# A linear-attention block with adaptive norm: the running sum and the modulation sums of the token loop go from VectorE to GpSimd and ScalarE

## The chip, the cores and the metric

The kernel runs on one core of a Trainium2 chip. What counts is the time of one execution on the device in microseconds; the median of several runs is given. A core has five engines that work side by side, each through its own list of instructions in order: TensorE (PE in the profile, its weight loads PEld), VectorE (DVE), ScalarE (ACT), GpSimd (POOL) and SyncE (SP, which here issues most of the DMAs). They wait for one another by semaphores.

## The reference, cut to what matters

There are 2048 tokens of width D = 512, in float32. A vector c gives six modulation vectors; a block of linear attention with 32 heads of 16 follows, then a bilinear feed-forward part.

```python
mod = (_silu(c) @ w_mod).reshape(c.shape[0], 6, 1, -1)
sa, ca, ga, sb, cb, gb = (mod[:, 0], mod[:, 1], mod[:, 2], mod[:, 3], mod[:, 4], mod[:, 5])
h = _layernorm(x, axis=-1) * (1 + ca) + sa
x = x + ga * _A_ref(h, A_wqkv, A_wo)
h = _layernorm(x, axis=-1) * (1 + cb) + sb
x = x + gb * _B_ref(h, B_w_gate, B_w_up, B_w_down)

# in _A_ref
phi = lambda t: jnp.where(t > 0, t + 1, jnp.exp(t)) + 1e-6
pq, pk = phi(q), phi(k)
kv = jnp.einsum("bhsd,bhse->bhde", pk, v)
z = jnp.einsum("bhsd->bhd", pk)
num = jnp.einsum("bhqd,bhde->bhqe", pq, kv)
den = jnp.einsum("bhqd,bhd->bhq", pq, z)[..., None] + 1e-6
```

Two sums matter here. z is the sum of phi(k) over all tokens. And each modulation vector is a product of silu(c), 512 long, with a 512x512 part of w_mod.

## The kernel before

The tokens are worked on in four chunks of 512, each of four tiles of 128 tokens by 512 columns, so sixteen tiles. Matrix products are made from pairs: a matrix is split into a high part, rounded to the format that TensorE takes, and a low part, the rest, and three matmuls (high by high, high by low, low by high) make one product. ScalarE writes most high parts, VectorE subtracts to get the low ones.

The kernel has a first part (norm and modulation of the first chunk), then a token loop, and then the attention's second half and the feed-forward part. The token loop goes over the tiles i = 4 to 15, after tiles 0 to 3 written out before it. In one step i of the loop

- TensorE makes the projection to k of tile i + 2 (`proj`, twelve matmuls of 128x512 on lines 219 to 221); the last two steps project q of tiles 4 and 5 instead, and step 4 also projects q of tile 3;
- ScalarE and VectorE split the normed x of tile i + 1 (`k_split_x`: xh, xl, lines 206 and 207) and its phi(k) (`k_split`: kh on line 363, kl on line 364);
- two of the first steps of each chunk transpose and modulate the next chunk (`transpose`, line 284; `modulated`, lines 302 to 307), whose pair h, l the later projections read;
- ScalarE and VectorE make phi(k) of tile i + 2 from the projection (`k_phi`, lines 327, 328 and 331);
- VectorE adds phi(k) of tile i + 1 to the running sum `zacc` (`z_add`, line 357; line 355 for the first);
- TensorE adds the products of tile i to four accumulators that stay in place over the whole loop (`t_tile`, lines 372 to 374, twelve matmuls of 128x512);
- and what `extra[i]` lists for this step: weight splits, loads, and the modulation vectors.

Modulation vectors 2 to 5 are made in the loop, beside the tokens. For vector v, `mod_load` fetches four pieces of w_mod of 128x512, and `mod_part(v, ...)` lets VectorE build the tile `accs[v]`: piece 0 times its column of silu(c) (line 178), then for pieces 1 to 3 a multiply and add (line 180). What remains is a sum over the 128 partitions, which TensorE makes: with ones as a column for vectors 3 and 4 (`mod_col`, line 185, then `col_out` on VectorE), or, for vectors 2 and 5, from a split pair with a block of ones (`mod_row`, line 195, copied out by ScalarE). After the last tile the running sum is split as well, and TensorE sums it over the partitions (`over_rows`, line 195). GpSimd's only work in the loop is the power that gives a chunk's reciprocal deviation (line 262); right after the loop it multiplies phi(q) by the summed z (line 712).

The order of instructions of each engine is the order in which the program writes them: the schedule is manual. Tiles of 128x512 come from one pool of 99 buffers, and an instruction that gets a buffer waits until the last reader of what was in it is done. Four PSUM banks serve the projections, transposes and column sums in turn, and four hold the accumulators.

Of the kernel before, what the change touches and what calls it, by code (L numbers as in the profile page):

```python
# [10 lines left out]
AF = mybir.ActivationFunctionType  # L11
ALU = mybir.AluOpType
# [10 lines left out]
def tile_adaln_block(  # L23
# [12 lines left out]
    nc = tc.nc  # L36
# [33 lines left out]
    def T(p, tag, shape=(P, D), dt=F32, bufs=None):  # L70
        cnt[0] += 1
        return p.tile(list(shape), dt, tag="t" if p is tiles else tag, name=f"{tag}_{cnt[0]}", bufs=bufs)

    def B(tag, shape=(P, D), dt=F32):

        return T(tiles, tag, shape, dt)
# [4 lines left out]
    def bank():  # L81
        return T(ps_w, "bank")
# [26 lines left out]
    def load(src, tag, by=None):  # L109
        raw = B(tag, (P, *src.shape[1:]))[:src.shape[0]]  # L110
        (by or nc.sync).dma_start(raw, src)
        return raw
# [44 lines left out]
    sc = consts.tile([P, KD], F32, name="sc")  # L157
# [14 lines left out]
    def mod_acc(acc, raws, ks, on=None):  # L172
        for k in ks:
            if k == 0:
                if on:
                    on.activation(acc, raws[k], AF.Copy, scale=sc[:, 0:1])
                else:
                    nc.vector.tensor_scalar(acc, raws[k], sc[:, 0:1], None, op0=ALU.mult)
            else:
                nc.vector.scalar_tensor_tensor(acc, raws[k], sc[:, k:k + 1], acc, op0=ALU.mult, op1=ALU.add)  # L180

    def mod_col(acc, ps):

        for b in range(KD):
            nc.tensor.matmul(ps[:, b:b + 1], acc[:, b * P:(b + 1) * P], ones, start=True, stop=True)
        return ps

    def col_out(v, ps, add):
        t = consts.tile([P, KD], F32, name=f"col{v}")
        nc.vector.tensor_scalar(t, ps[:, :KD], add, None, op0=ALU.add)  # L190
        return t

    def over_rows(ps, pair):
        for m, x in enumerate(pair):
            nc.tensor.matmul(ps, ones_r, x, start=m == 0, stop=m == 1)

    def mod_row(v, pair):
        ps = bank()
        over_rows(ps, pair)
        t = consts.tile([P, D], F32, name=f"row{v}")  # L200
        nc.scalar.activation(t, ps, AF.Copy)
        return t


    def split(src, h, l, low=None):
        nc.scalar.activation(h, src, AF.Copy)  # L206
        (low or nc.vector).tensor_tensor(l, src, f32(h), op=ALU.subtract)  # L207

    def split_raw(raw, shape=(P, D), low=None):
        h = B("w", shape, F32R)  # L210
        l = B("w", shape, F32R)
        split(raw, h[:raw.shape[0]], l[:raw.shape[0]], low)
        return h, l
# [99 lines left out]
    NT = NCH * NJ  # L313
    norm = [Norm(xts[0])]
    wk, wq, wv = [], [], []
    kx, phk, phq, q_ps = {}, {}, {}, {}
# [36 lines left out]
    def z_add(i):  # L353
        if i == 1:
            nc.vector.tensor_tensor(zacc, phk[0], phk[1], op=ALU.add)
        elif i > 1:
            nc.vector.tensor_tensor(zacc, zacc, phk[i], op=ALU.add)
        phk.pop(i - 1, None)

    def k_split(i):  # L360
# [23 lines left out]
    zacc = B("z")  # L384
# [188 lines left out]
    rows, cols = {}, {}  # L573
    accs = {}

    raw_m, raw_o, wo_s = {}, [], []
# [2 lines left out]
        raw_m.update({v: load_mod(v) for v in vs})  # L579

    def mod_part(v, *ks):
        if 0 in ks:
            accs[v] = B("f")
        mod_acc(accs[v], raw_m[v], ks)

    extra = {4: lambda: (wv.extend(split_raw(r) for r in raw_v[0:1]),),
             5: lambda: (wv.extend(split_raw(r) for r in raw_v[1:2]),),
             6: lambda: (wv.extend(split_raw(r) for r in raw_v[2:3]), mod_load(2),),
             7: lambda: (wv.extend(split_raw(r) for r in raw_v[3:4]),),
             8: lambda: (mod_part(2, 0, 1), mod_load(3)),  # L590
             9: lambda: (mod_part(2, 2, 3), mod_load(4)),
             10: lambda: (accs.update({2: split_raw(accs[2])}), mod_part(3, 0, 1, 2), mod_load(5)),
             11: lambda: (mod_part(3, 3), mod_part(4, 0, 1), rows.update({2: mod_row(2, accs[2])})),
             12: lambda: (raw_o.extend(load(wo_v[k], "raw") for k in range(KD)), mod_part(4, 2, 3), mod_part(5, 0), cols.update({3: col_out(3, mod_col(accs[3], bank()), 0.0)})),
             13: lambda: (mod_part(5, 1, 2, 3), wo_s.extend(split_raw(x) for x in raw_o[:1]), accs.update({5: split_raw(accs[5])}), cols.update({4: col_out(4, mod_col(accs[4], bank()), 1.0)})),
             14: lambda: (wo_s.extend(split_raw(x) for x in raw_o[1:]),), 15: lambda: rows.update({5: mod_row(5, accs[5])})}
    q_at = {4: 3}
    ahead = {}

# [15 lines left out]
    t_tile(1, *range(KD))  # L615
    qps2 = proj(2, wq)
    z_add(1)
    k_split_x(3)
    nx.transpose(0, 1)
# [5 lines left out]
    nx.transpose(2, 3)  # L625
    nx.modulated(ca, sa, 2, 3, cast=nc.vector)
    z_add(2)
    q_a(2, qps2)
    q_b(2)
    z_add(3)  # L630
    t_tile(3, *range(KD))
    ahead[4] = proj(4, wk)
# [971 lines left out]
```

## Time and profile before

| | |
|---|---|
| median of 3 runs | 554.61 us (554.56 to 554.82) |
| span of the profiled execution | 552.4 us, 2.2 us less than the median |
| TensorE matmuls, busy | 545.8 us (99%), granted clock 0.999 |
| TensorE weight loads | 460.1 us (83%) |
| VectorE | 432.2 us (78%) |
| ScalarE | 299.5 us (54%) |
| GpSimd | 176.8 us (32%) |
| stretch 88 to 122 us of the token loop | TensorE 34.00, VectorE 29.96, ScalarE 18.35, GpSimd 0.00 of 34.00 us |

The span goes from the first to the last instruction of the one execution that was profiled; the time of a run also holds what lies around it, 554.61 − 552.4 = 2.2 us. The token loop of steps 4 to 15 lies between about 55 and 127 us. Busy shares are averages over stages with different limits, so the stage of the change is read by itself. A line of a timeline gives the start in us, the duration, the engine, the line of the code, the operation, and what is written from what; in brackets stands how long the engine was idle before and what ended that. A line of groups gives the number of instructions, their busy time and the mean of one in ns, then the idle time before them. For a single line of the code the three numbers are the shortest, the median and the longest in ns.

### The profile page before, as it was taken

Reading aid. Unit: us, or ns where it says so; the run is one execution under the profiler, and the core shown is the slowest. Engines: PE = TensorE matmul, PEld = TensorE weight load, DVE = VectorE, ACT = ScalarE, POOL = GpSimd, SP = SyncE. Lnnn points to the kernel's source line nnn. Section 1 sums busy time; section 2 is a strip of 40 time slices with the busy share of each in tenths; the row PEclk is TensorE's granted clock in tenths of the full one; section 3 lists DMA queues with packets and bytes.
Section 4 is the critical chain, followed back from the end, with each engine's and each line's share of the span. In section 5 each row is a group of like instructions: output and inputs, shape, how many; then the busy total and the mean of one; then the engine's idle time right before and its main releaser. Section 6 shows DMA issues by size and latency. Waiting matters only on the chain. (4 is left out here: it accounts for less than half of the span.)

```text
span 552.4 us, 8146 instructions
## 1 busy us (share of the span) xinstructions
PE 545.8 (99%) x2775; PEld 460.1 (83%) x2775; DVE 432.2 (78%) x794; ACT 299.5 (54%) x535; POOL 176.8 (32%) x180
## 2 busy tenths in 40 slices
PE   8999999999999999999999999999999999999997
PEld 6888888888888888888888888878888888888886
DVE  6878779978998998865655767797577877879696
ACT  4876857456467876654545355463243534453540
POOL 2000000003527646353556644540002524242400
PEclk9999999999999999999999999999999999999999
DMA  8910224203230045195888634289786534342004
GB/s 256 373 57 1 76 77 152 77 0 77 78 115 2 0 154 189 39 316 180 285 286 274 222 123 163 87 312 391 231 259 218 173 131 138 129 146 86 1 0 153
DMA packets 58512, 83.24 MB, mean 151 GB/s; under 512 B 6564, under 2 KB 23720, under 8 KB 58472
## 3 DMA queue, kind: packets, MB, share of 16 engines
q1 hardware_dynamic: 56544, 81.16, 44.1%
q10 hardware_dynamic: 1928, 1.58, 0.9%
q8 instruction: 22, 0.36, 0.3%
q14 instruction: 18, 0.15, 0.1%
HBM read 53.02 MB, written 29.69 MB: 150 GB/s over the span
## 5 line engine op out<-in xcount | busy, mean ns | idle before, releaser
L1057 PE MATMUL bank<-h,w 128*128 128x512 f32 (+1 forms) x924 | 221.6, 391 | 0.2 <-POOL w L1020 0.2
L1057 PEld LDWEIGHTS bank<-h,w 128*128 128x128 f32 (+1 forms) x924 | 168.2, 186 | 36.2 <-POOL w L1020 0.6
L1063 ACT ACTIVATE bank<-bank 128x512 f32<-128x512 f32 (+2 forms) x46 | 26.2, 571 | 122.7 <-PE bank L1057 122.5
L1253 DVE TENSOR_TENSOR x<-acc,x 128x256 f32<-128x256 f32 x132 | 48.0, 414 | 13.7 <-PE acc L1226 13.1
L1226 PE MATMUL acc<-w,kh 128*128 128x256 f32 x308 | 57.1, 282 | 0.0
L1226 PEld LDWEIGHTS acc<-w,kh 128*128 128x128 f32 x308 | 50.6, 190 | 3.7
L1020 POOL TENSOR_TENSOR w<-raw,w 128x256 fp32r<-128x256 f32 (+3 forms) x22 | 24.7, 1121 | 73.7 <-ACT w L1013 64.1
L219 PE MATMUL bank<-w,h 128*128 128x512 f32 x112 | 44.1, 394 | 0.0
L221 PE MATMUL bank<-w,h 128*128 128x512 f32 x112 | 43.7, 390 | 0.0
L220 PE MATMUL bank<-w,h 128*128 128x512 f32 x112 | 43.6, 390 | 0.0
L1226 PE MATMUL acc<-w,kl 128*128 128x256 f32 x154 | 43.5, 283 | 0.0
L871 PE MATMUL acc<-w,xh 128*128 128x512 f32 x128 | 40.7, 399 | 0.0
L712 POOL TENSOR_TENSOR f<-h,zb 128x512 f32<-128x512 f32 x12 | 17.5, 1468 | 62.9 <-ACT zb L692 48.9
L262 POOL TENSOR_TENSOR rstd<-ve,half 128x4 f32<-128x4 f32 (+3 forms) x12 | 11.2, 935 | 81.4 <-DVE ve L259 68.0
L1083 DVE TENSOR_TENSOR phi<-bank,g 128x512 f32<-128x512 f32 (+1 forms) x22 | 15.1, 687 | 25.2 <-PE bank L1057 25.2
L1063 ACT ACTIVATE u<-bank 128x512 f32<-128x512 f32 (+1 forms) x44 | 26.1, 594 | 15.4 <-PE bank L1057 15.2
L1113 DVE TENSOR_TENSOR g<-bank,u 128x512 f32<-128x512 f32 (+1 forms) x22 | 15.2, 689 | 21.2 <-ACT u L1063 19.9
L1020 POOL TENSOR_TENSOR w<-t,w 128x512 fp32r<-128x512 f32 (+1 forms) x22 | 29.6, 1346 | 0.0
L1146 PE MATMUL acc<-w,kh 128*128 128x512 f32 (+1 forms) x76 | 29.6, 390 | 0.0
L1147 PE MATMUL acc<-w,kh 128*128 128x512 f32 (+1 forms) x76 | 29.6, 390 | 0.0
L1148 PE MATMUL acc<-w,kl 128*128 128x512 f32 (+1 forms) x76 | 29.6, 389 | 0.0
L277 ACT ACTIVATE n<-x,nmr,rstd 128x512 f32<-128x512 f32 x31 | 23.6, 808 | 10.9 <-DVE nmr L267 10.7
(204 smaller groups left out, 1187.0 us busy)
## 6 DMA issues: line engine op xcount, KB each, us to landing
right<-w SPq DMA_DIRECT2D x56, 256.0 KB, 3.7
w<-right SPq DMA_DIRECT2D x56, 256.0 KB, 4.3
x<-in_A_x_dram SPq DMA_DIRECT2D x22, 256.0 KB, 5.2
raw<-in_w_mod_dram SPq DMA_DIRECT2D x22, 256.0 KB, 3.7
raw<-in_B_w_down_dram SPq DMA_DIRECT2D x18, 256.0 KB, 3.0
side_s<-h SPq DMA_DIRECT2D x16, 256.0 KB, 2.6
h<-side_s SPq DMA_DIRECT2D x16, 256.0 KB, 5.3
raw<-in_A_wqkv_dram SPq DMA_DIRECT2D x12, 256.0 KB, 6.2
```

The lines of the kernel that those rows point to most:

```text
L219: nc.tensor.matmul(ps, ah, bh, start=begin and i == 0, stop=False)
L220: nc.tensor.matmul(ps, ah, bl, start=False, stop=False)
L221: nc.tensor.matmul(ps, al, bh, start=False, stop=end and i == n - 1)
L871: nc.tensor.matmul(yps[i], x, y, start=fresh and k + n == 0, stop=k == KD - 1 and n == 2, skip_group_check=True)
L1020: sub = lambda out, x, y: (on or nc.gpsimd).tensor_tensor(out, x, f32(y), op=ALU.subtract)
L1057: mm = lambda x, y, **kw: nc.tensor.matmul(ps, x[:, k], y, skip_group_check=True, **kw)
L1063: nc.scalar.activation(out, x, AF.Copy)
L1146: nc.tensor.matmul(dn[j], hh[:n, a:b], dh[:n], start=i == 0, stop=False)
L1147: nc.tensor.matmul(dn[j], hh[:n, a:b], dl[:n], start=False, stop=False)
L1148: nc.tensor.matmul(dn[j], hl[:n, a:b], dh[:n], start=False, stop=i == n_of - 1)
L1226: mm = lambda x, y, **kw: nc.tensor.matmul(ps, x[:, a:b], y, skip_group_check=True, **kw)
L1253: nc.vector.tensor_tensor(xt[:, halves[at]], banks[b][m], xt[:, halves[at]], op=ALU.add)
```

## The change

The addition to the running sum goes to GpSimd for tiles 5 to 13; tiles 1 to 4, 14 and 15 stay on VectorE. Each of the sixteen modulation pieces (four vectors of four) is multiplied by ScalarE into a tile of its own; the first piece's tile becomes `accs[v]`, and GpSimd adds the other three to it, twelve additions in all. The split of `accs[5]` moves from step 13 to step 14 of the loop, behind the weight splits of that step.

```diff
         elif i > 1:
-            nc.vector.tensor_tensor(zacc, zacc, phk[i], op=ALU.add)
+            on = nc.gpsimd if 4 < i < NT - 2 else nc.vector
+            on.tensor_tensor(zacc, zacc, phk[i], op=ALU.add)
...
     def mod_part(v, *ks):
-        if 0 in ks:
-            accs[v] = B("f")
-        mod_acc(accs[v], raw_m[v], ks)
+
+        for k in ks:
+            part = B("f")
+            nc.scalar.activation(part, raw_m[v][k], AF.Copy, scale=sc[:, k:k + 1])
+            if k:
+                nc.gpsimd.tensor_tensor(accs[v], accs[v], part, op=ALU.add)
+            else:
+                accs[v] = part
...
-             13: lambda: (mod_part(5, 1, 2, 3), wo_s.extend(split_raw(x) for x in raw_o[:1]), accs.update({5: split_raw(accs[5])}), cols.update({4: col_out(4, mod_col(accs[4], bank()), 1.0)})),
-             14: lambda: (wo_s.extend(split_raw(x) for x in raw_o[1:]),), 15: lambda: rows.update({5: mod_row(5, accs[5])})}
+             13: lambda: (mod_part(5, 1, 2, 3), wo_s.extend(split_raw(x) for x in raw_o[:1]), cols.update({4: col_out(4, mod_col(accs[4], bank()), 1.0)})),
+             14: lambda: (wo_s.extend(split_raw(x) for x in raw_o[1:]), accs.update({5: split_raw(accs[5])})), 15: lambda: rows.update({5: mod_row(5, accs[5])})}
```

## The prediction

> **What bounds the kernel now.** I read four views: the page's busy times, the list of waits of TensorE, the table by stretch of the token loop, and then the order of time around the places where TensorE takes a result of VectorE just after it is made. First the page.
>
> ```profile
> span 552.4 us, 8146 instructions
> PE 545.8 (99%) x2775; PEld 460.1 (83%) x2775; DVE 432.2 (78%) x794; ACT 299.5 (54%) x535; POOL 176.8 (32%) x180
> ```
>
> TensorE is busy for all but 552.4 − 545.8 = 6.6 us. Busy time of a pipelined engine can hide short stalls, so the waits and the start times have to confirm it. These are all the waits of TensorE's matmuls that the trace lists:
>
> ```profile
> PE acc L153 <- DVE w L148: 2.0, 1, 2.0
> PE bank L295 <- ACT n L277: 0.6, 1, 0.6
> PE bank L1057 <- POOL w L1020: 0.2, 1, 0.2
> ```
>
> None is on a line of the token loop (projections L219 to L221, products of the sum L372 to L374). The loop, over the two stretches that the change touches. After the length stand the busy us and instructions of PE (TensorE's matmuls), PEld, DVE (VectorE), ACT (ScalarE) and POOL (GpSimd), then TensorE's granted clock, the DMA share and GB/s:
>
> ```profile
> 56.00:88.00 32.00, 32.00 (x154) 26.62 (x153) 25.01 (x48) 25.07 (x41) 1.24 (x2) 1.00 0.31 99
> 88.00:122.00 34.00, 34.00 (x163) 28.38 (x163) 29.96 (x52) 18.35 (x31) 0.00 (x0) 1.00 0.19 62
> ```
>
> The reader should see TensorE at 34.00 of 34.00 us at a granted clock of 1.00, although VectorE is at 29.96. VectorE is crowded but it is not what TensorE waits for. Now the start times of two projections, each of 12 matmuls of 128x512 (first row of each, and the row that follows its last):
>
> ```profile
> 96.87 0.39 PE L219 MATMUL bank<-w,h 128*128 128x512 f32 x1
> ...
> 99.59 0.39 PE L372 MATMUL acc<-kh,xh 128*128 128x512 f32 x1
> ...
> 102.78 0.40 PE L219 MATMUL bank<-w,h 128*128 128x512 f32 x1
> ...
> 105.54 0.39 PE L372 MATMUL acc<-kh,xh 128*128 128x512 f32 x1
> ```
>
> (99.59 − 96.87)/12 = 0.227 us from start to start, (105.54 − 102.78)/12 = 0.230. So hidden stalls are at most some 0.04 us in a projection. In this loop TensorE sets the time, and work taken from VectorE is taken from beside it.
>
> **What is removed.** Nine of the fifteen additions of the running sum (tiles 5 to 13), and sixteen modulation products, leave VectorE:
>
> ```profile
> L357 DVE TENSOR_TENSOR z<-z,phi 128x512 f32<-128x512 f32 x14 | 9.5, 682 | 0.0
> L180 DVE SCALAR_TENSOR_TENSOR f<-raw,sc,f 128x512 f32<-128x512 f32 x12 | 9.0, 750 | 0.3
> ...
> L178 DVE TENSOR_SCALAR f<-raw,sc 128x512 f32<-128x512 f32 x4 | 1.9, 482 | 0.0
> ```
>
> 9 × 0.682 + 9.0 + 1.9 = 17.0 us. On the path: 0, because no matmul of the loop waits for VectorE.
>
> **What is added on ScalarE.** Sixteen scaled copies of 128x512. The trace has no such copy in that shape, only these neighbours: a plain copy, and an activation with a scale and a bias from SBUF.
>
> ```profile
> L206 ACT ACTIVATE xh<-n x15: 613/616/631, 31.6 to 142.0; 128x512 fp32r<-128x512 f32 x15
> ```
> ```profile
> L277 ACT ACTIVATE n<-x,nmr,rstd 128x512 f32<-128x512 f32 x31 | 23.6, 808 | 10.9 <-DVE nmr L267 10.7
> ```
>
> One operand from SBUF instead of none or two: between 0.616 and 0.808, I take the middle, 0.71; sixteen make 9.9 to 12.9, taken as 11.4 us. All fall behind the activation at 86.49 us that is quoted below, where ScalarE would go from 18.35 to about 29.7 of 34 us (31.3 at the upper end). It fits. What lies behind a product on ScalarE is the next tile's split and the exponentials; they cost nothing while the free time in that stretch covers them.
>
> **What is added on GpSimd.** Twenty-one additions (9 of the sum, 12 of the products) of two 128x512 operands. The nearest row has the same shape:
>
> ```profile
> L712 POOL TENSOR_TENSOR f<-h,zb x12: 1277/1306/1837, 125.9 to 215.4; 128x512 f32<-128x512 f32 x12
> ```
>
> 1.306 as a rule, 1.837 at worst: 27.4 us, up to 38.6. GpSimd is nearly empty here (1.24 and 0.00 us above). Seventeen of them fall in the stretch of 34 us (sum tiles 9 to 13 and the twelve): 22.2 us, at worst 31.2. It fits, but the consumers on TensorE have to be looked at one by one.
>
> **The new waits.** TensorE takes the columns of vector 4 in loop step 13, and the row of vector 5 in step 15; these are the latest additions against the earliest use.
>
> ```profile
> 86.49 0.63 ACT L328 ACTIVATE phi<-phi 128x512 f32<-128x512 f32 x1
> ...
> 121.79 1.66 ACT L206 ACTIVATE w<-raw 128x512 fp32r<-128x512 f32 x3
> ```
> ```profile
> 114.66 0.95 PE L185 MATMUL bank<-ones,f 128*128 128x1 f32 x8
> ...
> 127.00 0.62 PE L195 MATMUL bank<-w,ones_r 128*128 128x512 f32 x2
> ```
> ```profile
> 122.53 1.89 DVE L207 TENSOR_TENSOR w<-raw,w 128x512 fp32r<-128x512 f32 x3
> ```
>
> The first two products stand behind the activation of 86.49 and are done at 87.12 + 2 × 0.71 = 88.5. From there to the last addition of vector 4 GpSimd has 13 additions: 9 of products (an addition for each of k = 1 to 3 of vectors 2, 3 and 4) and 4 of the sum (tiles 10 to 13). At the worst duration, one straight after the other, they end at 88.5 + 13 × 1.837 = 112.4, before 114.66. The three of vector 5 then end at 117.9. Its split was moved to step 14: on ScalarE it stands behind the three weight copies that end at 123.45, so GpSimd is done 5 us before. On VectorE its low half follows the three that end at 124.42 and takes 0.69 more: 125.1, against a use at 127.00. Vectors 2 and 3 end earlier in the same queue; a split of vector 2 that waits for GpSimd holds up ScalarE, behind it the next products and the split of the next tile, whose use is one loop step (105.54 − 99.59 = 5.95 us) later. VectorE's addition for tile 14 now waits for GpSimd's for tile 13, the eleventh of the 13, done by 88.5 + 11 × 1.837 = 108.7 at worst; in the order of the program it comes after phi of tile 15, whose row follows.
>
> ```profile
> 113.43 0.69 DVE L331 SCALAR_TENSOR_TENSOR phi<-bank,phi 128x512 f32<-128x512 f32 x1 [1.99 <-ACT phi L328]
> ```
>
> So it finds its operand ready by 5 us; were it late, the rest of step 13 on VectorE would stand behind it. Cost of all these waits: 0.
>
> **The two tight places.** VectorE's results reach TensorE with the least to spare here: the low half of phi(k) of tile 8, and the low half of the last chunk's fourth block (first its making, then the first matmul that reads it).
>
> ```profile
> 80.55 0.68 DVE L364 SCALAR_TENSOR_TENSOR kl<-phi,kh 128x512 fp32r<-128x512 f32 x1
> ...
> 92.66 0.69 DVE L307 TENSOR_TENSOR h<-f,h 128x512 fp32r<-128x512 f32 x1
> ```
> ```profile
> 81.91 0.39 PE L374 MATMUL acc<-kl,xh 128*128 128x512 f32 x1
> ...
> 93.93 0.39 PE L221 MATMUL bank<-w,h 128*128 128x512 f32 x1
> ```
>
> To spare: 81.91 − 81.23 = 0.68 us and 93.93 − 93.35 = 0.58. Both have sum additions of VectorE ahead of them that go (tiles 6 and 7 before the first; tile 9 and two products, 0.68 + 0.48 + 0.75 = 1.9 us, before the second), so left alone they gain room. But GpSimd now runs at the same time, and the trace shows what that does to VectorE:
>
> ```profile
> 180.99 1.28 POOL L1020 TENSOR_TENSOR w<-t,w 128x512 fp32r<-128x512 f32 x1
> ```
> ```profile
> 181.05 1.27 DVE L735 TENSOR_TENSOR den<-den,den 128x32 f32<-128x32 f32 x1
> ```
> ```profile
> L735 DVE TENSOR_TENSOR den<-den,den x12: 191/194/1270, 156.5 to 231.0; 128x32 f32<-128x32 f32 x12
> ```
>
> An addition of 0.194 us took 1.270 and ended 0.05 us after GpSimd's instruction: it had been held until GpSimd was through. The price of one encounter is between 0 (it falls beside an instruction that is not held) and 1.28. Most of VectorE's work in the loop reads two SBUF operands, so I count half an instruction of GpSimd, 0.64, for each of the two that can meet VectorE ahead of each place: 1.28. Against it stand the room of 0.68 + 2 × 0.68 = 2.0 and 0.58 + 1.9 = 2.5. Stall taken: 0. If each encounter costs a whole 1.28 and nothing were gained before: 2 × 1.28 − 0.68 = 1.9 and 2 × 1.28 − 0.58 = 2.0, together 3.9 us; this is the upper end.
>
> The same rows give a second upper end, by the stretch instead of the place. Of 88 to 122 us, 9.0 + 1.9 + 5 × 0.68 = 14.3 us leave VectorE, and if each of the 17 additions holds it for a whole 1.28, 21.8 come back: 29.96 − 14.3 + 21.8 = 37.5 of 34 us, so the loop would end 3.5 us later.
>
> The Trainium skill, SBUF — State Buffer, section "Who interferes with whom", has this as a rule: a VectorE instruction with two SBUF inputs and a GpSimd instruction that reads SBUF exclude each other for the whole of the one that came first. The row of 1.270 agrees with it. By the rule at its hardest the sum would be the 3.5 us of the stretch, by the rows at half an encounter it is 0.
>
> **Buffers.** Twelve more tiles of the pool of 99 are taken, so later loads get other buffers, and a load waits until its buffer's last reader is through. The SP queue shows such a wait ahead of the loads of the feed-forward weights (line 994; total, times, longest), and TensorE its first matmul on what is made of them:
>
> ```profile
> SPq L994 <- PE bank L221: 31.6, 2, 31.2
> ```
> ```profile
> 206.08 1.52 PE L1057 MATMUL bank<-h,w 128*128 128x512 f32 x6
> ```
>
> The loop ends near 127 us, so a load that comes some us later is covered by most of 80 us. Cost 0; if this cover were gone it would show as a wait on line 1057.
>
> **The sum.** Removed on the path 0, added on the path 0. The profiled execution has a span of 552.4, the median of the runs is 554.61, so 2.2 us lie around the span. Taken to the median: 554.6 us.
>
> **Rivals.** *Held VectorE (slower).* GpSimd's additions hold VectorE ahead of the two tight places. It decides once VectorE is held there for longer than 2.0 or 2.5 us. For it: the row of 1.270, and VectorE's crowding. Against it: near the first place GpSimd has only the additions of tiles 7 and 8, and in the second stretch 0.64 instead of 1.28 an encounter gives 29.96 − 14.3 + 10.9 = 26.6 of 34 us. Time: 554.6 + 3.9 = 558.5 if both places are lost in full, 554.6 + 3.5 = 558.1 by the stretch, about 556 if one place is half lost. The rule cited above is this case.
> *Faster pace.* A freer VectorE lets the matmuls start at 0.227 instead of 0.230 everywhere: twelve projections and twelve sums of 12 matmuls, 288 × 0.003 = 0.9 us at most: 553.7. Against it: nothing ties the slower pace to VectorE, and the pace of 0.227 was reached in the same crowded stretch.
> *No relief.* VectorE gets back by being held what it loses in work (17.0 against 21 × 0.64 = 13.4): its busy time then hardly falls, and the time stays at 554.6 all the same.
>
> **How the numbers follow.** No path changed (with or without relief): 0.86, 554.6, own range 554.1 to 555.2. Held VectorE beyond the room: 0.11, 555.7 to 558.5. Faster pace: 0.03. A change under 0.2% (1.1 us) is about what a measurement of this kernel can't tell from none. So faster 0.03, same 0.86, slower 0.11. The range reaches 0.5 us below and, for one half-lost tight place, 1.3 us above: 554.1 to 555.9.
>
> **What would show it.** In the profile after, TensorE's waits should still name no line of the loop, its busy time should be 34.00 of 34.00 in the same stretch, VectorE's there should fall well below 29.96, ScalarE's rise to some 30 and GpSimd's to 22 or more. A group of two-operand instructions on VectorE that takes 1.2 us and more would show the holding. The prediction is wrong if TensorE waits for VectorE before L374 of tile 8 or L221 of tile 12's projection, or for GpSimd before L185 or L195, or if the wait on line 1057 grows.

## The result and the profile after

The change made the kernel slower: 556.19 us median (555.16 to 556.67) against 554.3 (553.5 to 554.82), a ratio of 1.0036 with a 95% interval of 1.0026 to 1.0047, so 2.0 us (1.4 to 2.6). The forecast of 554.6 and its range up to 555.9 were too low. First the page and TensorE's waits in the kernel after (the line numbers moved by one to six; 1057 is now 1063, 357 is 358, 364 is 365).

```profile
span 553.6 us, 8169 instructions
PE 546.3 (99%) x2775; PEld 460.2 (83%) x2775; DVE 434.2 (78%) x769; ACT 309.2 (56%) x551; POOL 206.1 (37%) x201
```
```profile
PE acc L153 <- DVE w L148: 2.0, 1, 2.0
PE bank L221 <- DVE h L307: 1.0, 1, 1.0
PE bank L284 <- ACT n L277: 0.2, 1, 0.2
```

VectorE has 25 instructions fewer and is busy for 2.0 us more. TensorE has two new waits, both in the token loop: one for the low half of the last chunk (L307, the second tight place of the forecast) and one for normed x (L277), which the forecast did not list. The same two stretches of the loop as before, in the same columns:

```profile
56.00:88.00 32.00, 31.84 (x153) 26.31 (x152) 24.15 (x43) 25.22 (x42) 7.47 (x7) 1.00 0.26 82
88.00:122.00 34.00, 33.04 (x157) 27.11 (x156) 28.29 (x29) 26.44 (x44) 23.78 (x16) 1.00 0.23 78
```

TensorE is no longer busy throughout. In the second stretch VectorE does 29 instructions instead of 52 in 28.29 us instead of 29.96: part of what it keeps takes twice as long. The groups of VectorE there show it (the two that were 0.68 each):

```profile
L207 DVE TENSOR_TENSOR xl<-n,xh 128x512 fp32r<-128x512 f32 x6 | 8.5, 1421 | 2.6 <-ACT xh L206 2.6
L365 DVE SCALAR_TENSOR_TENSOR kl<-phi,kh 128x512 fp32r<-128x512 f32 x6 | 8.5, 1412 | 0.0
```

The loss can be dated by two matmuls that every one of these kernels has, the first of tile 4's projection and the first for the row of vector 5 (of before, the second stands in the prediction). First before, then after:

```profile
46.87 0.39 PE L219 MATMUL bank<-w,h 128*128 128x512 f32 x1
```
```profile
46.67 0.39 PE L219 MATMUL bank<-w,h 128*128 128x512 f32 x1
...
128.53 0.62 PE L195 MATMUL bank<-w,ones_r 128*128 128x512 f32 x2
```

127.00 − 46.87 = 80.13 us became 128.53 − 46.67 = 81.86. I call this the loop's length below: the loop is 1.73 us longer, within the 1.4 to 2.6 us of the times. (The two profiled spans differ by less, 553.6 − 552.4 = 1.2 us, because TensorE makes up 0.5 us later; the last section shows where.) Where it began is seen in the order of time of VectorE, GpSimd, ScalarE and TensorE between 76 and 84 us of the kernel after:

```profile
76.20 1.23 DVE L267 SCALAR_TENSOR_TENSOR nmr<-mv,rstd 128x4 f32<-128x4 f32 x1 [0.59 <-POOL rstd L262]
```
```profile
76.14 1.28 POOL L358 TENSOR_TENSOR z<-z,phi 128x512 f32<-128x512 f32 x1
```
```profile
77.47 1.52 ACT L277 ACTIVATE n<-x,nmr,rstd 128x512 f32<-128x512 f32 x2 [4.17 <-DVE nmr L267]
```
```profile
83.26 0.77 PE L284 MATMUL bank<-ident,n 128*128 128x128 f32 x5 [0.16 <-ACT n L277]
```

Before, line 267 and the two lines of VectorE that matter further on stood so:

```profile
77.06 0.16 DVE L267 SCALAR_TENSOR_TENSOR nmr<-mv,rstd 128x4 f32<-128x4 f32 x1
```
```profile
89.94 0.68 DVE L207 TENSOR_TENSOR xl<-n,xh 128x512 fp32r<-128x512 f32 x1
90.54 0.68 DVE L364 SCALAR_TENSOR_TENSOR kl<-phi,kh 128x512 fp32r<-128x512 f32 x1
91.15 0.42 DVE L304 CAST h<-f 128x512 fp32r<-128x512 f32 x1
```

Line 267 is a product of 128x4, 0.16 us long before. GpSimd's power for chunk 3 ends, and its end releases two things: line 267 on VectorE, which waits for it, and, in GpSimd's own queue, the addition of tile 7. GpSimd is first by 0.06 us, and line 267 ends 0.01 us after GpSimd's addition: 76.20 + 1.23 = 77.43 against 77.42. ScalarE's normed x waits for line 267, TensorE's transposes for ScalarE. The first product of the sum behind these transposes starts 83.61 − 46.87 = 36.74 us into the loop before and 83.78 − 46.67 = 37.11 after: the first loss is 0.37 us (before, then after):

```profile
83.61 0.47 PE L372 MATMUL acc<-kh,xh 128*128 128x512 f32 x1
```
```profile
83.78 0.48 PE L373 MATMUL acc<-kh,xh 128*128 128x512 f32 x1
```

The rest, 1.73 − 0.37 = 1.36 us, is lost at tile 12's projection. On VectorE and TensorE, after:

```profile
89.12 1.36 DVE L207 TENSOR_TENSOR xl<-n,xh 128x512 fp32r<-128x512 f32 x1
90.40 1.78 DVE L365 SCALAR_TENSOR_TENSOR kl<-phi,kh 128x512 fp32r<-128x512 f32 x1
...
93.68 1.58 DVE L307 TENSOR_TENSOR h<-f,h 128x512 fp32r<-128x512 f32 x1
```
```profile
93.98 0.39 PE L220 MATMUL bank<-w,h 128*128 128x512 f32 x1
95.32 0.50 PE L221 MATMUL bank<-w,h 128*128 128x512 f32 x1 [0.96 <-DVE h L307]
```

There three instructions that take 0.68 or 0.69 alone take 1.36, 1.78 and 1.58: 2.7 us of holding, and 95.32 − 93.98 = 1.34 us between two matmuls that stand 0.23 apart before.

VectorE comes to line 207 only 89.94 − 89.12 = 0.82 us earlier than before, although 1.78 us of its work just ahead are gone (88.16 to 89.94 before: tile 9's addition and two products). GpSimd adds tile 9 as soon as its phi(k) is there, at 83.37, and holds the split of a weight for 1.46 − 0.69 = 0.77 us; another 0.2 is the later end of line 267. The first two lines are of before, the others of after:

```profile
83.55 0.69 DVE L207 TENSOR_TENSOR w<-raw,w 128x512 fp32r<-128x512 f32 x1
...
88.16 0.68 DVE L357 TENSOR_TENSOR z<-z,phi 128x512 f32<-128x512 f32 x1
```
```profile
83.37 1.30 POOL L358 TENSOR_TENSOR z<-z,phi 128x512 f32<-128x512 f32 x1 [4.58 <-DVE phi L331]
...
83.75 1.46 DVE L207 TENSOR_TENSOR w<-raw,w 128x512 fp32r<-128x512 f32 x1 [0.53 <-ACT w L206]
...
87.24 1.32 ACT L586 ACTIVATE f<-raw,sc 128x512 f32<-128x512 f32 x2
...
88.47 0.62 ACT L206 ACTIVATE xh<-n 128x512 fp32r<-128x512 f32 x1
```

ScalarE's xh, which line 207 needs as well, is ready no sooner, at 88.47 + 0.62 = 89.09: two of the products now stand ahead of it.

### The profile page after: what moved, and what is told of

The parts are those of the page before. It is cut to its first block, busy times and chain, and to the rows that moved or that the text cites. A ratio compares the mean times of both kernels' runs of the same rounds, so it can differ in the third digit from the quotient of the medians.

```text
span 553.6 us, 8169 instructions
## 1 busy us (share of the span) xinstructions
PE 546.3 (99%) x2775; PEld 460.2 (83%) x2775; DVE 434.2 (78%) x769; ACT 309.2 (56%) x551; POOL 206.1 (37%) x201
## 3 DMA queue, kind: packets, MB, share of 16 engines
q10 hardware_dynamic: 1928, 1.58, 0.9%
## 4 chain that ended last, share of the span: by engine, by line
PE 92%; DVE 4%; ACT 3%; issue 1%; POOL 0%; POOLq 0%; DVEq 0%
PE bank L1063 38%; PE acc L1232 10%; PE acc L877 8%; PE bank L221 4%; PE bank L219 4%; PE bank L220 3%; PE acc L1152 3%; PE acc L1153 3%; PE acc L1154 3%; PE acc L373 2%; PE acc L374 2%; PE acc L375 2%; PE acc L460 2%; PE bank L284 1%; PE acc L153 1%; ACT n L277 1%
## 5 line engine op out<-in xcount | busy, mean ns | idle before, releaser
L1026 POOL TENSOR_TENSOR w<-t,w 128x512 fp32r<-128x512 f32 (+1 forms) x22 | 29.7, 1349 | 0.0
L277 ACT ACTIVATE n<-x,nmr,rstd 128x512 f32<-128x512 f32 x31 | 23.6, 808 | 10.6 <-DVE nmr L267 10.4
L1232 PEld LDWEIGHTS acc<-w,kl 128*128 128x128 f32 x154 | 29.3, 191 | 0.0
```

Of the source, the lines that this page charges most:

```text
L1026: sub = lambda out, x, y: (on or nc.gpsimd).tensor_tensor(out, x, f32(y), op=ALU.subtract)
L1232: mm = lambda x, y, **kw: nc.tensor.matmul(ps, x[:, a:b], y, skip_group_check=True, **kw)
```

## The experiments

Theory 1: GpSimd's additions hold VectorE's instructions, and the loss comes where one is held ahead of something TensorE soon needs. Theory 2: the products on ScalarE stand ahead of the splits and delay them. Each table row below gives the time as a ratio to the kernel before on the same chip (95% interval), and the loop's length from the two matmuls named above, less the 80.13 us of before.

| kernel | ratio of times | loop longer by, us |
|---|---|---|
| the change, first and second time | 1.0036 (1.0026 to 1.0047), 1.0034 (1.0019 to 1.005) | 1.73, 1.78 |
| running sum only | 1.0042 (1.002 to 1.0063) | 1.10 |
| products only | 1.0007 (0.9997 to 1.0016) | 0.00 |
| products by ScalarE, additions by VectorE | 1.0008 (0.9999 to 1.0017) | −0.03 |
| before, with 21 spare additions | 1.0211 (1.0197 to 1.0225) | 10.67 |
| before, with 21 spare one-operand products | 1.0098 (1.0072 to 1.0125) | 3.70 |
| before, with 63 spare fills | 1.0015 (1.0005 to 1.0025) | 0.66 |
| tile 7 back on VectorE | 1.0 (0.9991 to 1.0009) | −0.04 |
| tile 10 back on VectorE | 1.0014 (1.0005 to 1.0022) | 0.36 |
| both back | 1.0007 (0.9993 to 1.0021) | −0.08 |
| all on GpSimd, nmr ahead of tile 7 | 0.9996 (0.9987 to 1.0005) | −0.05 |

**The running sum alone.** The first two edits are the halves of the change.

```diff
-            nc.vector.tensor_tensor(zacc, zacc, phk[i], op=ALU.add)
+            on = nc.gpsimd if 4 < i < NT - 2 else nc.vector
+            on.tensor_tensor(zacc, zacc, phk[i], op=ALU.add)
```

> Only the running sum of tiles 5 to 13 goes to GpSimd; the modulation products stay on VectorE. Theory 1, GpSimd's two-operand additions hold VectorE's: the addition of tile 7 holds the small nmr instruction (line 267, 1.2 us instead of 0.16) and costs TensorE about 0.35 us at the transposes of step 8; at tile 12's projection VectorE's relief of 0.6 us and its room of 0.58 about pay for one held instruction. So 0.3 to 0.8 us slower than before. Theory 2, the products on ScalarE delay the splits: there are none, so the same as before (within 0.2 us).

Line 267 is held again, and the loop is longer by 1.10 us, more than theory 1's upper 0.8; theory 2's "same" is out. The medians, 555.43 against 553.99, are 1.44 us apart; the ratio of 1.0042 has a wide interval. 0.37 us are lost at the transposes again, the other 0.7 at tile 12's projection, where GpSimd's addition of tile 10 holds line 180 (1.65 us instead of 0.75) ahead of the last chunk's low halves.

```profile
76.43 1.24 DVE L267 SCALAR_TENSOR_TENSOR nmr<-mv,rstd 128x4 f32<-128x4 f32 x1 [0.58 <-POOL rstd L262]
```

**The products alone** (`mod_part` of the change, the sum as before).

> Only the modulation products go to ScalarE and their additions to GpSimd; the whole running sum stays on VectorE. Theory 1: nmr is not held (0.16 us) and the transposes of step 8 do not wait; the additions of vector 2 meet VectorE ahead of tile 12's projection, so TensorE waits there for 0.3 to 1.3 us. Theory 2: the products alone make the whole loss, 1.5 to 2 us.

The loop has exactly the length of before, 126.94 − 46.81 = 80.13 us. So twelve additions on GpSimd, and VectorE held at ten places, cost nothing; this misses theory 1's 0.3 to 1.3 as well as theory 2's 1.5 to 2. Line 267 is not held here, and neither is line 364 of tile 10, for whose addition GpSimd is not used; the kernels with single additions undone, below, tell the two apart.

```profile
76.99 0.16 DVE L267 SCALAR_TENSOR_TENSOR nmr<-mv,rstd 128x4 f32<-128x4 f32 x1
```

**ScalarE's products without GpSimd.**

```diff
-                nc.gpsimd.tensor_tensor(accs[v], accs[v], part, op=ALU.add)
+                nc.vector.tensor_tensor(accs[v], accs[v], part, op=ALU.add)
```
(and the running sum as before)

> The products are made by ScalarE, but VectorE makes the additions and the whole running sum, so GpSimd has nothing new. Theory 1: no instruction of VectorE is held, no wait of TensorE in the loop, the time of before within 0.3 us. Theory 2: as slow as the change, 1.5 to 2 us over before, with TensorE waiting at tile 12's projection.

TensorE has no wait in the loop, and no instruction of VectorE there is longer than in the kernel before. Theory 2 is out.

**Spare work on GpSimd beside all of before's work.**

```diff
             nc.vector.tensor_tensor(zacc, zacc, phk[i], op=ALU.add)
+            if 4 < i < NT - 2:
+                nc.gpsimd.tensor_tensor(spare, phk[i], phk[i], op=ALU.add)
...
         mod_acc(accs[v], raw_m[v], ks)
+        for k in ks:
+            if k:
+                nc.gpsimd.tensor_tensor(spare, raw_m[v][k], raw_m[v][k], op=ALU.add)
```

> The kernel before with all of its work where it was, and 21 more additions on GpSimd (into a tile that nothing reads) at the places where the change has them: phi of tiles 5 to 13, and one for each of k = 1 to 3 of the four vectors, each of two operands of 128x512. Theory 1: VectorE is held without any relief, so the loss is at least that of the change, 2 to 5 us. Theory 2: ScalarE has nothing new, so the same as before.

It lost 10.67 us of loop, more than twice the upper end expected: VectorE had 29.96 of 34 us to do, is held at some twenty places and is then busy for 33.69. Not all of the loss is waiting. Behind the wait of 2.6 us TensorE's granted clock is 0.50 between 99 and 102 us (1.00 in the kernel before), and its matmuls start 0.43 us apart instead of 0.23; that makes about 1.8 of the 10.67 us. The run says that GpSimd's additions alone are enough, with ScalarE as before. Its largest new waits of TensorE:

```profile
PE bank L219 <- DVE h L304: 2.6, 1, 2.6
...
PE acc L376 <- DVE kl L366: 1.0, 1, 1.0
```

The next two keep the places and change the operation: `tensor_scalar(spare, ..., 2.0, None, op0=ALU.mult)` instead of the addition, and three `memset(spare, 0.0)`.

> The kernel before with 21 extra instructions on GpSimd as in the run with spare additions, but each of one 128x512 operand (times 2.0) instead of two. If GpSimd holds VectorE's two-operand instructions whenever it reads SBUF: VectorE's instructions are held by up to the length of a one-operand instruction, and the loss falls with that length (5 to 10 us if it is 0.7 us against 1.3). If only GpSimd's two-operand instructions hold: no loss, VectorE's line 207 stays at 0.68 us.

> The kernel before with 63 extra fills of a 128x512 tile on GpSimd (three at each of the 21 places; they read nothing and wait for nothing but GpSimd's own order, so most follow one another from about 57 and 77 us on). If the holding is about reads of SBUF, VectorE's lines 207, 357 and 364 keep 0.68 us while GpSimd fills and the time is that of before. If it is about writes too, some dozens of VectorE's instructions are held and TensorE waits.

The one-operand kernel lost 3.70 us in the loop, less than the 5 to 10 expected, although its instructions last 1.49 us and not 0.7. In its profile the loop also starts 2.05 us late (48.92 instead of 46.87), ahead of any instruction of the edit, with a granted clock of 0.74 between 10 and 15 us; and there are only two runs of it. A group and an instruction of it, and two instructions of VectorE in the kernel with the fills:

```profile
L590 POOL TENSOR_SCALAR z<-raw x12: 1491/1538/2057, 88.0 to 118.6; 128x512 f32<-128x512 f32 x12
```
```profile
79.57 0.57 DVE L267 SCALAR_TENSOR_TENSOR nmr<-mv,rstd 128x4 f32<-128x4 f32 x1
```
```profile
90.57 0.68 DVE L207 TENSOR_TENSOR xl<-n,xh 128x512 fp32r<-128x512 f32 x1
...
93.02 0.68 DVE L304 CAST h<-f 128x512 fp32r<-128x512 f32 x1
```

With one operand to read, GpSimd holds line 267 for 0.57 − 0.16 = 0.41 us. Under fills, which read nothing, two-operand instructions keep 0.68, as expected; the time of before was missed all the same. The cast of line 304, 0.42 us long otherwise, takes up to 0.68, and the product of line 178, 0.48 otherwise, up to 0.88. Nothing else on VectorE is held there, so line 307 comes at 93.74 instead of 92.66, and the loop is 0.66 us longer. The forecast's page of the Trainium skill, SBUF — State Buffer, section "Who interferes with whom", says the same: a VectorE instruction with two SBUF inputs contends with a GpSimd instruction that reads SBUF and not with one that only writes it, while a cast or a `tensor_scalar` on VectorE can run in a two-port mode, which contends with GpSimd. These runs agree with it on who is held. They differ on how long: by the page the second one waits until the first is done, but line 267 was let go after 0.57 us, in an operation of GpSimd that lasts 1.49 at least, and no instruction of VectorE was held for more than 0.5 us in that loop.

**One addition undone at a time.** The edit for tile 7; for tile 10 the tuple is `(10,)`, for both `(7, 10)`.

```diff
-            on = nc.gpsimd if 4 < i < NT - 2 else nc.vector
+            on = nc.gpsimd if 4 < i < NT - 2 and i not in (7,) else nc.vector
```

> The change with one addition undone: the running sum takes tile 7 on VectorE again. Theory 1: GpSimd has no addition behind the power of chunk 3, so line 267 takes 0.16 us instead of 1.23, the transposes of step 8 do not wait, and TensorE gains the 0.38 us that it loses there in the change; the loss of 1.36 us at tile 12's projection stays. So 0.3 to 0.5 us faster than the change. If the holding is not what costs, as slow as the change.

> The change with one addition undone: the running sum takes tile 10 on VectorE again (behind the low halves of the last chunk in its order). Theory 1: line 365 of tile 10 is not held (1.12 us less), the low half of the fourth block is made before the next addition of GpSimd starts, and TensorE's loss at tile 12's projection falls from 1.36 us to 0 to 0.3; the 0.38 us at the transposes of step 8 stay. So 1.0 to 1.4 us faster than the change, 0.4 to 0.8 over before. If the count of held time alone mattered, about a fifteenth of the loss would go.

> Both additions undone (tiles 7 and 10 on VectorE), seven of nine and all twelve product additions still on GpSimd. Theory 1: TensorE waits nowhere in the loop and its matmuls come as in the kernel before (within 0.2 us at the loop's end); the time of before within 0.3 us, although VectorE is still held at some ten other places. Otherwise the loss falls only in step with the additions, by 2 of 21.

> The change once more, beside the three above on the same chip: TensorE 1.5 to 1.8 us later at the end of the loop than in the kernel before, 1.5 to 2.3 us slower in the time; the same instructions held at the same two places (line 267 of chunk 3; lines 207, 365 and 307 ahead of tile 12's projection).

The change once more lost 1.78 us of loop. Tile 7 alone took back everything, at both places: my expectation that 1.36 us would stay at tile 12's projection was wrong. Of that kernel, VectorE:

```profile
76.44 0.16 DVE L267 SCALAR_TENSOR_TENSOR nmr<-mv,rstd 128x4 f32<-128x4 f32 x1
...
88.30 1.37 DVE L207 TENSOR_TENSOR xl<-n,xh 128x512 fp32r<-128x512 f32 x1
89.59 1.77 DVE L365 SCALAR_TENSOR_TENSOR kl<-phi,kh 128x512 fp32r<-128x512 f32 x1
...
92.86 0.69 DVE L307 TENSOR_TENSOR h<-f,h 128x512 fp32r<-128x512 f32 x1
```

GpSimd still has an addition behind the power, that of tile 8, which the expectation overlooked. It waits for VectorE's addition of tile 7, starts 0.09 us behind line 267, and does not hold it:

```profile
76.53 1.29 POOL L358 TENSOR_TENSOR z<-z,phi 128x512 f32<-128x512 f32 x1
```

Line 267 ends at 76.60 instead of 77.43. Twelve us later lines 207 and 365 still start 0.82 and 0.81 us earlier and are held just as in the change. But line 307 starts at 92.86, ahead of GpSimd's next addition; in the change it starts at 93.68, behind it. The addition in tile 7's kernel and in the change:

```profile
93.17 3.25 POOL L588 TENSOR_TENSOR f<-f,f 128x512 f32<-128x512 f32 x2 [2.36 <-ACT f L586]
```
```profile
93.32 3.10 POOL L588 TENSOR_TENSOR f<-f,f 128x512 f32<-128x512 f32 x2 [1.69 <-ACT f L586]
```

So in tile 7's kernel it is VectorE that is first, and line 307 is not held. The two losses of the change are one delay. It is 0.83 us by each profile's own time and 1.07 from the first matmul of tile 4's projection (46.91 in tile 7's kernel, 46.67 in the change), which is as long as line 267 is held. It costs 0.36 at once, as tile 10's kernel shows by itself, and the rest where it lets GpSimd get ahead of line 307. Tile 10 back takes away the second loss only, as expected and by another way: line 365 is not held there. Its loop is 127.39 − 46.90 = 80.49. Both back give no more than tile 7 alone.

**Everything on GpSimd, and line 267 out of the way.** The product nmr of chunk 3 is made by GpSimd right behind the power, in front of tile 7's addition.

```diff
-            nx2.rstd_of()
+            nx2.rstd_of(aside=True)
...
-            nx2.nmr_of()
```

> The change with all of its additions on GpSimd, but chunk 3's small product nmr is made by GpSimd right behind the power, ahead of the addition of tile 7, so VectorE has no instruction there that can be held. If one held instruction of VectorE at that place makes both losses, TensorE waits neither at the transposes of step 8 nor at tile 12's projection, and the loop ends within 0.2 us of the kernel before; time within 0.4 us of before. If the number of additions on GpSimd counts, as slow as the change (1.5 to 2 us over before).

```profile
76.58 0.20 POOL L264 TENSOR_TENSOR nmr<-nm,rstd 128x4 f32<-128x4 f32 x1
76.73 2.67 POOL L358 TENSOR_TENSOR z<-z,phi 128x512 f32<-128x512 f32 x2
```

All 21 additions stay on GpSimd and the loss is gone: 0.9996, the loop 127.09 − 47.01 = 80.08 us. VectorE is still held at 16 places for about 13 us together (the sum of what its instructions last over their shortest time, 50 to 128 us; about 15 in the change, at 16 places too). This version does not beat the kernel before; TensorE has no wait left in the loop to remove.

## Why the prediction was wrong, step by step

- *What bounds the loop*: right. TensorE waited for nothing before, and taking 17 us from VectorE gained nothing in any version; the best ones have the loop's length of before within 0.08 us.
- *ScalarE's products at 0.71*: right. Fifteen of them in the stretch took 708 ns each, and ScalarE went to 26.44 of 34 us, below the 29.7 expected. They cost nothing by themselves (0.00 and −0.03 us).
- *GpSimd's additions, and the new waits of lines 185 and 195*: right in the outcome. In the second stretch they took 1.42 (products) and 1.74 us (sum) in the mean, within 1.306 to 1.837, and TensorE waited for none of them. The end called the worst for vector 5, 117.9, was not: its additions ended at 115.67 + 4.69 = 120.36, because they waited for ScalarE's products, and there was room for that too.
- *The two tight places*: this step failed. It put the stall at 0, and the loop lost 0.37 us at the transposes and 1.36 at tile 12's projection. It went wrong in three ways. It looked only for the last producer ahead of TensorE (lines 364 and 307), not for the small one that starts the chain: line 267, 77.06 + 0.16 in the trace, on which normed x hangs, and with it VectorE's work up to line 307, some 16 us later. It counted GpSimd's additions of tiles 7 and 8 as near line 364, which they did not hold. It priced an encounter at half of GpSimd's instruction, as if they met at random; here one event releases both. GpSimd was the first by 0.06 or 0.07 us in all six profiles where an instruction of it that reads and waits for nothing else stands behind the power of chunk 3, and in the four in which it is the sum's addition, line 267 pays 1.07 or 1.08 us, all but 0.2 of that addition's length. And it counted two encounters ahead of line 307, 1.28 us, where three came, 2.7 us.
- *The room against it*: too large. 2.5 us were to stand against the second place, 1.9 of it the work taken from VectorE. VectorE got to line 207 only 0.82 us sooner by the profile's time, about 1.0 against TensorE. The step left out a fourth encounter: it put tile 9's addition where VectorE had made it, at 88.16, but GpSimd makes it at 83.37 and took back 0.77 us there. The rest is the delay through line 267.
- *The rivals*: the one that came true, VectorE held, was named with the right mechanism, second place and sign, and given 0.11; its 3.9 us were the upper end. The sign that it named came, a wait of TensorE ahead of line 221 in tile 12's projection. The second upper end counted holding in bulk, by the stretch. In the change bulk decides little: ten held places in the products alone cost 0.00 us, and sixteen with nmr on GpSimd −0.05. It counts once VectorE has no free time left, as with the spare additions. *No relief* was right about VectorE's busy time, 28.29 us against 29.96, and wrong that the time stays.
- *Buffers*: right, no wait on line 1063 remains.

## What to carry to other kernels

An engine that is off the critical path may still own the one small instruction from which the next stage hangs, so before giving work to GpSimd look for VectorE's two-operand instructions that the same event releases: an addition queued on GpSimd right behind a short operation was ahead of VectorE's reader of that operation in all six profiles here. Place it behind that reader, or let GpSimd make the small product itself. Count room on the chain that feeds an instruction, with every encounter on it and at the time at which GpSimd will make its part, not by the work taken away alone, and follow a delay past the first place that absorbs part of it.

## What was not expected of the hardware

A one-operand `tensor_scalar` of 128x512 took GpSimd 1.49 us at least, more than its two-operand additions at their usual length (1.28 to 1.31). And holding goes both ways. Some 225 us after the loop, TensorE makes up 0.5 us against the kernel before, in the change and in all three kernels with tiles back, and not in the halves of the change or with nmr on GpSimd. At that place GpSimd meets a run of VectorE's two-operand instructions, in the kernel before and in tile 7's kernel:

```profile
353.24 2.93 POOL L1207 TENSOR_TENSOR t<-raw 128x256 f32<-128x256 f32 x1 [5.02 <-DVE raw L1280]
```
```profile
353.24 1.12 POOL L1213 TENSOR_TENSOR t<-raw 128x256 f32<-128x256 f32 x1 [5.02 <-DVE raw L1286]
```

The first is held behind several instructions of VectorE in a row, the second behind one, and the wait of line 1057 for GpSimd is gone with it. What decides it, with the same start to 0.01 us, stays open, and no run tried it by itself; it is too small to tell in the times.
